# Threshold attention and a squared-ReLU layer on one core: own step orders for the first three attention periods, and another place for the unread transposes

## The chip, the cores and the metric

The kernel runs on one core of one Trainium2 chip. The metric is the device time of one execution in microseconds. Three timed runs of the kernel before gave 1300.67, 1300.70 and 1300.83 us, median 1300.7.

## The reference

The inputs are q, k and v of shape (8, 8, 576, 64), a threshold tau of 0.02, and two weight matrices, which arrive as 64-bit floats. All else is fp32.

```python
scores = (1 / sqrt(64)) * q @ k.T
thresh = max(scores, axis=-1) - tau
scores = where(scores >= thresh, scores, -1e9)
attn = exp(scores - max(scores));  attn /= sum(attn) + 1e-9
x = (attn @ v) transposed to (8*576, 8*64)          # 4608 x 512
h = maximum(x @ w_in, 0)                            # w_in: 512 x 2048
out = (h * h) @ w_out                               # w_out: 2048 x 512
```

## The kernel before

The program has three stages, one after the other: attention (to about 504 us), the layer with w_in (L827) and the layer with w_out (L962). The two layers multiply with seven block products on two levels instead of eight, and PE is their pace. The change lies in the first stage alone.

**Units and periods.** Batch and pair of heads give 32 pairs. Four blocks of 128 query rows and, for two pairs together, one of 64 + 64 rows make 144 units; a period handles two units, A and B, so periods 0 to 71 have scores, and the loop runs some on either side. The steps of a period are named by short words, and a list of these words is the order in which they are recorded (the loop `for name in CONVERTING if converts(p) else PLAIN`, L697). Every engine takes its instructions in the recorded order, and semaphores hold an instruction until what it needs is there; no scheduler moves anything (`tc.manual_schedule()`). Periods 0 and 1 use PLAIN; CONVERTING holds from period 2, while the weights are turned from 64 to 32 bits, chunk by chunk.

**The steps.** In the order in which one unit's data goes through them:

- T: PE transposes queries or keys of a later pair into two PSUM banks (L397); eT: ACT copies them out (L402, L410).
- SA, SB: PE's score products (L434), those of unit A with the 64 last keys of both units, and those of unit B, into banks of the tile `sc`.
- topA1 and the like: DVE copies the scores to SBUF and finds each row's extreme (the sign is turned with the queries) (L452); two per unit, one for each head. The text calls them tops.
- leastA, leastB: POOL adds tau (L459). powA0 and the like: ACT's exponential (L462). maskA0 and the like: DVE drops what is under the threshold and sums the rest (L467).
- over (POOL, L474), inv (DVE, L477), spread (POOL, L517): the reciprocal of the sum, widened for a transposition.
- V, U, W: PE transposes the attention weights (L379) of the period before or of the one before that; eV, eU, eW: ACT copies them out (L524).
- PV: PE's product with v (L533); x, xs: DVE, ACT and POOL scale and copy it (L640, L642, L657), and SP writes it to DRAM (L579).
- fetch and c1 to c6: SP's load of a weight chunk (L191) and its conversion: ACT (L205, L211), POOL (L218, L245), DVE (L226, L234).

**Banks.** `sc` has six PSUM banks, the tile `pt` the other two. T writes bank 1 and bank 4 of `sc`, where the scores of the last 64 keys lie as well, W writes banks 2 and 3. A helper, `touch`, makes two engines that use the same bank wait for each other in recorded order, and frees those that use different ones. `pt` has one buffer, so each use of it waits until the one before has been copied out.

**Unread transposes.** `keep_busy(times)` (L1008) records transposes of the identity into a new `pt` tile that nobody reads (L1013). There are 15 before the first queries are transposed, 8 before the first keys are, and 20 after period 0. The 8 and the queries before them share `pt`, and so the 8 wait until ACT has copied the queries out.

**Loads.** SP issues nearly all DMAs, in recorded order; each one waits for the one eight before it. A load of keys of a later pair is recorded with eT, behind the transposes that free its buffer.

Of the kernel before, what the change touches and what calls it, by code (L numbers as in the profile page):

```python
# [10 lines left out]
FP32 = mybir.dt.float32  # L11
# [37 lines left out]
def kernel(  # L49
# [25 lines left out]
    nc = tc.nc  # L75
    B, H, S, D = q.shape
    P = 128
# [7 lines left out]
    BANK = 512  # L85
# [19 lines left out]
    ident = const.tile([P, P], FP32, name="ident")  # L105
# [375 lines left out]
    def do(n, what, *args):  # L481
        if n in soft:
            soft[n][what](*args)
# [4 lines left out]
    for g in range(2, 2 * len(pairs)):  # L488
        two, x = divmod(g - 4, 4)
# [9 lines left out]
    def fill(m, f, pt, at=None):  # L499

        first, count = FILLS[f]
        if m not in wT:
            wT[m] = sb.tile([P, (2 * CH + 2) * P], FP32, tag="wT", bufs=W_RING, name="wT")
        for i, (u, c) in enumerate(FIRST[first : first + count]):
            half_turn(pt, i, weights[2 * m + u][:, c, :, :].rearrange("p j d -> p (j d)"), at)
        if f == "W":
            for j in range(2):
                half_turn(pt, count + j, wT[m][:, ts(SCALE_AT + j, P)], at)

    def widen(m):  # L510

        if m not in wT:
            wT[m] = sb.tile([P, (2 * CH + 2) * P], FP32, tag="wT", bufs=W_RING, name="wT")
        one = smalls.pop(m)[:, 3, 0:1]
        wide = bass.AP(tensor=one.tensor, offset=one.offset, ap=[one.ap[0], [1, 2], [2, 2], [0, D]])
        to = wT[m][:, ds(SCALE_AT * P, 2 * P)].rearrange("p (j u d) -> p j u d", j=2, u=2)
        nc.gpsimd.tensor_copy(out=to, in_=wide)  # L517
# [42 lines left out]
    def has(n):  # L560
        return 0 <= n < NU
# [22 lines left out]
    def converts(p):  # L584
        return is_wide and (has_chunk(p) or has_chunk(p - 1))

    def has_chunk(p):
        return p in starts

    def begun(n):  # L590
        return starts.get(n)

    PLAIN = """
        fetch U SA topA1 over s1 s2 topA0 SB topB1 inv eU powA1 V topB0 leastA spread PV powA0 maskA1 leastB maskA0 eV T powB1 x maskB1 powB0 xs maskB0 eT W eW
    """.split()
    CONVERTING = """
        fetch c1 T SA topA1 c3 topA0 U eU powA1 SB topB0 over topB1 powA0 c4 powB0 PV eT inv leastA maskA1 x powB1 leastB spread V eV maskA0 W maskB0 c5 c6 eW maskB1 xs c2
    """.split()

    def spots():  # L600
        return [(sc[:, ds(b * BANK + REST, (FULL + 1) * HALF)], b * BANK) for b in (1, 4)]

# [3 lines left out]
    def period(p):  # L606

        A, B_, a, b = 2 * p, 2 * p + 1, 2 * p - 2, 2 * p - 1
        m, turns = p - 2, TURNS.get(p, ())
        late, pt = {"W": []}, {}  # L610

        def fills(f, m):
            if has(2 * m):
                pt[f] = pt_pool.tile([P, 2, BANK], FP32, tag="pt", name="pt")
                fill(m, f, pt[f])

        def evict(f, m):
            if has(2 * m):
                filled(m, f, pt[f], 2 * BANK if f == "W" else None)

        def W():
            if has(2 * m + 2):
                pt["W"] = middle()
                fill(m + 1, "W", pt["W"], 2 * BANK)

        def turn_some():
            late["turn"] = [turn(g // 2, g % 2, spots()) for g in turns]

        def PV():
            if has(2 * m):  # L630
                values(m)

        def given_out():
            if has(2 * m):
                x = sb.tile([P, 2, P], FP32, tag="x", bufs=2, name="x")
                by_vector = (0,)
                for j in range(2):
                    by = sc[:, ds(5 * j * BANK, P)], wT[m][:, ts(SCALE_AT + j, P)]
                    if j in by_vector:
                        made = nc.vector.tensor_tensor(out=x[:, j, :], in0=by[0], in1=by[1], op=ALU.mult)  # L640
                    else:
                        made = nc.scalar.copy(x[:, j, :], by[0])  # L642
                    touch("x", made, 5 * j * BANK, P, m)
                late["x"] = x, [j for j in range(2) if j not in by_vector], wT[m]
                wT.pop(m)
                valued(m)

        def scaled_x():
            if has(2 * m):
                x, js, by = late["x"]  # L650
                if len(js) == 2:
                    nc.gpsimd.tensor_tensor(
                        out=x[:, :, :].rearrange("p j q -> p (j q)"), in0=x[:, :, :].rearrange("p j q -> p (j q)"),
                        in1=by[:, ds(SCALE_AT * P, 2 * P)], op=ALU.mult,
                    )
                for j in js if len(js) == 1 else ():
                    nc.gpsimd.tensor_tensor(out=x[:, j, :], in0=x[:, j, :], in1=by[:, ts(SCALE_AT + j, P)], op=ALU.mult)  # L657
                give_x(m, x)
            ask(False)

        def scored_a():
            if has(A):
                scores(A, False)
                scores(A, True)
                scores(B_, True)
                softmax(A)

        def scored_b():
            if has(A):
                scores(B_, False)  # L670
                softmax(B_)

        def every(key):
            for then in late.get(key, ()):
                then()

        steps = {
            "U": lambda: fills("U", m), "V": lambda: fills("V", m + 1), "W": W, "T": turn_some,
            "eU": lambda: evict("U", m), "eV": lambda: evict("V", m + 1), "eW": lambda: evict("W", m + 1),
            "eT": lambda: every("turn"),  # L680
            "SA": scored_a, "SB": scored_b,
            "PV": PV, "x": given_out, "xs": scaled_x,
            "c1": lambda: convert1(begun(p)), "c2": lambda: convert2(begun(p)),
            "c3": lambda: convert3(begun(p - 1)), "c4": lambda: convert4(begun(p - 1)),
            "c5": lambda: convert5(begun(p - 1)), "c6": lambda: convert6(begun(p - 1)),
            "s1": lambda: sums_due(p) and sums_step(), "s2": lambda: sums_due(p) and p % 2 == 0 and sums_step(), "fetch": lambda: fetch(begun(p + 2)),
        }
        steps["spread"] = lambda: has(2 * m + 2) and widen(m + 1)
        steps["over"] = lambda: do(a, "over")
        steps["inv"] = lambda: do(a, "inverse")  # L690
        for letter, n in (("A", A), ("B", B_)):
            for what, name in (("least", "least"),):
                steps[what + letter] = lambda n=n, name=name: do(n, name)
            for what, name in (("top", "top"), ("pow", "power"), ("mask", "mask")):
                for j in range(2):
                    steps[f"{what}{letter}{j}"] = lambda n=n, name=name, j=j: do(n, name, j)
        for name in CONVERTING if converts(p) else PLAIN:  # L697
            steps[name]()
        for n in (A, B_):
            if has(n) and units[n][1] == FULL:  # L700
                for i in units[n][0]:
                    turned.pop(i)
# [301 lines left out]
    with tc.manual_schedule():  # L1004
        with ExitStack() as stack:
            sc = stack.enter_context(tc.tile_pool(name="sc", bufs=1, space=PSUM)).tile([P, 6 * BANK], FP32, name="sc")
            pt_pool = stack.enter_context(tc.tile_pool(name="pt", bufs=1, space=PSUM))

            def keep_busy(times):

                pt = pt_pool.tile([P, 2, BANK], FP32, tag="pt", name="idle")
                for _ in range(times):
                    nc.tensor.transpose(pt[:, 0, 0:P], ident[:, :], ident[:, :])  # L1013

            load_q(0)
            load_k(0)
            read_tau()
            first = sb.tile([P, 4, 4], FP32, tag="small", bufs=4, name="small")
            nc.scalar.activation(out=first[:, 0, :], in_=ident[:, 0:4], func=AF.Exp)
            load_v(0)  # L1020
            keep_busy(15)
            pq = pt_pool.tile([P, 2, BANK], FP32, tag="pt", name="pq")
            turn(0, 0, [(pq[:, r, :], None) for r in range(2)])()
            keep_busy(8)
            turn(0, 1, spots(), nc.vector.tensor_copy)()
            for i in range(1, 3):
                load_v(i)
            for p in range(-2, NU // 2 + 3):
                period(p)
                if p == 0:  # L1030
                    keep_busy(20)
                if X_FIRST <= p < X_FIRST + 4:
                    load_x(0, XPARTS[p - X_FIRST :][:1])
                if p == X_FIRST + 4:
                    summing.append(prepare_x(0, lambda op, out, x, y: op(nc.gpsimd, out, x, y)))
            for _ in range(60):
                sums_step()
            ask()
# [186 lines left out]
```

## Time and profile before

One execution was profiled. Its own time is 1300.85 us, its span from the first to the last instruction 1299.1 us.

| | PE | PEld | DVE | ACT | POOL |
|---|---|---|---|---|---|
| busy us | 1260.8 | 1124.5 | 996.1 | 854.3 | 909.0 |
| share of the span | 97% | 87% | 77% | 66% | 70% |

PE is TensorE's matmuls and transposes, PEld its weight loads, DVE the vector engine, ACT the scalar engine, POOL GpSimd and SP the engine that issues DMAs. In rows of groups and of the order of time, the number in brackets is the engine's idle time before the row and what released it. A product of fp32 operands shows two records in the trace, a transpose one. The clock column is the share of TensorE's full speed that the throttle granted; it shows 1.00 ahead of the first record of the clock, which stands at 13.75 us, whatever the speed was there.

### The profile page before, as it was taken

To read this page: it belongs to the slowest core of one execution; us is meant where nothing else is said; L and a number is where in the kernel's file an instruction comes from. 1 tells how busy PE (TensorE), PEld (TensorE's weight loads), DVE (VectorE), ACT (ScalarE), POOL (GpSimd) and SP (SyncE) were. 2 spreads that over 40 slices of the span, in tenths; PEclk is the share of its full clock that TensorE was granted. 3 is DMA by queue.
4 is the path that set the end of the run, shared out by engine and by line. 5 is a ranking of instruction groups with operands and counts; after the bars stand their busy time and mean duration, and the time that the engine had idled before them with its cause. 6 is when DMAs were issued, how large, how long until landed. Compare 5 with 4: busy or idle time off the path is not lost.

```text
span 1299.1 us, 46337 instructions
## 1 busy us (share of the span) xinstructions
PE 1260.8 (97%) x18619; PEld 1124.5 (87%) x18619; DVE 996.1 (77%) x2425; ACT 854.3 (66%) x1536; POOL 909.0 (70%) x1102
## 2 busy tenths in 40 slices
PE   7999999999999999999999999999999999999998
PEld 4666666666766668999999999999999999999998
DVE  4999999999999995877787778777646654665463
ACT  4999999999999994757675766575523432343240
POOL 1566565566666663977897789768777867777775
PEclk8999999999999999999999999999999999999999
DMA  5465567534433322556655665479645324522411
GB/s 139 121 164 151 155 193 193 152 92 102 96 80 88 88 61 69 170 183 221 199 167 184 214 209 166 160 273 396 219 160 163 94 74 159 163 81 88 159 34 33
DMA packets 247031, 192.03 MB, mean 148 GB/s; under 512 B 97184, under 2 KB 195488, under 8 KB 246816
## 3 DMA queue, kind: packets, MB, share of 16 engines
q1 hardware_dynamic: 245360, 188.63, 48.2%
q8 instruction: 146, 2.39, 0.8%
q14 instruction: 69, 0.57, 0.2%
q10 hardware_dynamic: 1456, 0.44, 0.1%
HBM read 116.65 MB, written 72.35 MB: 145 GB/s over the span
## 4 chain that ended last, share of the span: by engine, by line
PE 60%; DMA 2%; ACT 1%; DVE 0%; issue 0%; POOL 0%; ACTq 0%; SPq 0%
PE ph L827 29%; PE po L962 29%; DMA wall<-w 1%; PE sc L533 1%; PE sc L434 1%; DMA g<-arena 0%; PE pt L379 0%; ACT arena L806 0%; ACT arena L807 0%; DVE arena L452 0%; POOL arena L122 0%; ACT arena L524 0%; ACT c L773 0%; DVE arena L467 0%; PE sc L379 0%
## 5 line engine op out<-in xcount | busy, mean ns | idle before, releaser
L125 POOL TENSOR_TENSOR arena<-arena 128x512 f32<-128x512 f32 (+1 forms) x314 | 377.6, 1221 | 124.7 <-DVE arena L125 110.1
L962 PE MATMUL po<-wall,arena 128*128 128x128 f32 x3528 | 394.7, 275 | 1.4 <-ACT arena L739 1.4
L962 PEld LDWEIGHTS po<-wall,arena 128*128 128x128 f32 x3528 | 394.2, 192 | 1.8 <-ACT arena L739 1.8
L827 PE MATMUL ph<-arena,wall 128*128 128x128 f32 x3528 | 394.2, 275 | 0.5 <-DVE arena L640 0.5
L827 PEld LDWEIGHTS ph<-arena,wall 128*128 128x128 f32 x3528 | 394.0, 192 | 0.6 <-ACT arena L642 0.6
L125 DVE TENSOR_TENSOR arena<-ph,arena 128x512 f32<-128x512 f32 x378 | 256.4, 689 | 86.3 <-PE ph L827 65.9
L122 POOL TENSOR_TENSOR arena<-arena 128x128 f32<-128x128 f32 (+2 forms) x314 | 254.6, 812 | 50.9 <-DMA arena<-w 34.6
L462 ACT ACTIVATE arena<-arena 128x576 f32<-128x576 f32 x288 | 223.0, 850 | 23.3 <-DVE arena L452 23.1
L125 DVE TENSOR_TENSOR arena<-po,arena 128x128 f32<-128x128 f32 x378 | 108.3, 290 | 168.1 <-PE po L962 164.0
L467 DVE SCALAR_TENSOR_TENSOR arena<-arena 128x576 f32<-128x576 f32 x288 | 227.1, 817 | 2.7 <-POOL arena L459 2.0
L452 DVE TENSOR_SCALAR_CACHE_REDUCE arena<-sc 128x576 f32<-128x576 f32 x288 | 203.9, 750 | 19.8 <-ACT arena L524 7.1
L773 ACT COPY c<-arena 128x512 f32<-128x512 f32 (+1 forms) x303 | 173.6, 580 | 49.8 <-DVE arena L122 41.3
L533 PEld LDWEIGHTS sc<-arena 64*64 64x64 f32 x5760 | 144.7, 133 | 47.5 <-DVE arena L452 44.6
L122 DVE TENSOR_TENSOR arena<-arena,c 128x512 f32<-128x512 f32 (+1 forms) x267 | 174.9, 663 | 5.7 <-ACT c L773 4.0
L434 PE MATMUL sc<-arena 64*64 64x64 f32 (+1 forms) x2304 | 171.5, 422 | 5.2 <-ACT arena L402 3.4
L533 PE MATMUL sc<-arena 64*64 64x128 f32 (+1 forms) x5760 | 160.7, 262 | 12.8 <-DVE arena L452 9.4
L524 ACT COPY arena<-pt 128x1024 f32<-128x1024 f32 x144 | 156.4, 1086 | 5.2 <-PE pt L379 5.1
L739 ACT COPY arena<-po 128x128 f32<-128x128 f32 x63 | 16.6, 264 | 186.5 <-PE po L962 183.7
L379 PEld LDWEIGHTS pt<-ident,arena 64*128 64x128 f32 x2304 | 83.4, 139 | 43.2 <-ACT arena L524 34.5
L739 ACT COPY arena<-ph 128x512 f32<-128x512 f32 x63 | 36.6, 581 | 122.6 <-PE ph L827 122.0
L434 PEld LDWEIGHTS sc<-arena 64*64 64x64 f32 x2304 | 60.9, 135 | 55.0 <-issue 28.4
L379 PE MATMUL pt<-ident,arena 64*128 64x64 f32 x2304 | 101.2, 228 | 3.8 <-ACT arena L524 3.3
(47 smaller groups left out, 944.3 us busy)
## 6 DMA issues: line engine op xcount, KB each, us to landing
g<-arena SPq DMA_DIRECT2D x144, 256.0 KB, 2.4
arena<-g SPq DMA_DIRECT2D x144, 256.0 KB, 4.5
w<-arena SPq DMA_DIRECT2D x60, 256.0 KB, 2.3
wall<-w SPq DMA_DIRECT2D x49, 256.0 KB, 5.3
arena<-w SPq DMA_DIRECT2D x44, 256.0 KB, 4.1
arena<-in_v_dram SPq DMA_DIRECT2D x32, 288.0 KB, 3.8
out_dram<-arena SPq DMA_DIRECT2D x70, 128.0 KB, 2.2
arena<-in_q_dram SPq DMA_DIRECT2D x64, 128.0 KB, 3.8
```

The source lines that it names most:

```text
L122: e.tensor_tensor(out=out, in0=x, in1=y, op=ALU.subtract)
L125: e.tensor_tensor(out=out, in0=x, in1=y, op=ALU.add)
L379: made = nc.tensor.transpose(pt[:, r, ts(slot, HALF)], of[rows, :], ident[rows, rows])
L434: made = nc.tensor.matmul(sc[at, ds(to, count)], lhs, kT[rows, ds(at_k, count)], start=True, stop=True)
L452: made = nc.vector.tensor_scalar(out=s[:, j, :], in0=sc[:, ds(at, S)], scalar1=1.0, scalar2=None, op0=ALU.mult, op1=ALU.min, accum_out=nmx ...
L462: nc.scalar.activation(out=w[:, :, j, :], in_=of(j), func=AF.Exp, bias=nmx[:, j : j + 1], scale=-1.0)
L467: nc.vector.scalar_tensor_tensor(out=w[:, :, j, :], in0=of(j), scalar=thr[:, j : j + 1], in1=w[:, :, j, :], op0=ALU.is_le, op1=ALU.mult, a ...
L524: touch("weights", nc.scalar.copy(joined(to), whole(pt, 0, count)), at, 2 * BANK, m)
L533: made = nc.tensor.matmul(sc[ds(u * D, D), ds(5 * j * BANK + row, count)], loaded_v[i][rows, (c - (u != j)) % CH, :], wT[m][rows, ds(weigh ...
L773: nc.scalar.copy(c, y)
L827: nc.tensor.matmul(to[:, j, :], W_IN[m, k][:, ts(j, P)], of[k][:, m - 1, :], start=(not more and j == 0), stop=True, skip_group_check=True,)
L962: nc.tensor.matmul(to, g[:, j, :], w[:, j, :], start=(not more and j == 0), stop=(j == 3), skip_group_check=True)
```

## The change

The first three periods get lists of their own (`FIRSTS`). The words id4, id8 and id14 are new steps that record so many unread transposes inside a period, in a `pt` tile; the lists use id4 and id14 in period 0 and id4 twice in period 1. The 20 after period 0 are gone. In the opening, the unread transposes go to bank 2 of `sc` (`unread`) instead of `pt`: 15 as before, 6 in place of 8, and 4 new ones between the first keys' transposes and period 0.

In the lists themselves: periods 0 and 1 record T ahead of the period's last top (the old list has it behind unit A's masks), period 1 records SB ahead of the second top and the weight load last instead of first, period 2 records c2 near its start and c1 at its end instead of the reverse, and the masks and thresholds stand in other orders. No other period changes, and the same work is done in each.

```diff
+    FIRSTS = {
+        0: """
+            SA SB id4 fetch topA1 topA0 powA1 leastA powA0 topB1 T id14 powB1 topB0 powB0 eT maskA0 leastB maskA1 maskB1 maskB0
+        """.split(),
+        1: """
+            SA topA1 SB topA0 id4 topB0 over inv powA1 V eV spread T powA0 topB1 eT W id4 leastA maskA1 leastB powB1 maskA0 maskB1 powB0 maskB0 fetch eW
+        """.split(),
+        2: """
+            T SA fetch c2 U topA1 c3 over eU SB powA1 topA0 c4 powA0 c5 topB0 powB0 leastA topB1 eT maskA1 PV inv powB1 V leastB x spread maskA0 eV maskB1 maskB0 W eW xs c6 c1
+        """.split(),
+    }
...
+        for times in (4, 8, 14):
+            steps[f"id{times}"] = lambda times=times: keep_busy(times)
...
-        for name in CONVERTING if converts(p) else PLAIN:
+        for name in FIRSTS.get(p) or (CONVERTING if converts(p) else PLAIN):
...
-            def keep_busy(times):
+            def keep_busy(times, to=None):
 
-                pt = pt_pool.tile([P, 2, BANK], FP32, tag="pt", name="idle")
+                if to is None:
+                    to = pt_pool.tile([P, 2, BANK], FP32, tag="pt", name="idle")[:, 0, 0:P]
                 for _ in range(times):
-                    nc.tensor.transpose(pt[:, 0, 0:P], ident[:, :], ident[:, :])
+                    nc.tensor.transpose(to, ident[:, :], ident[:, :])
+
+            unread = sc[:, ds(2 * BANK, P)]
...
-            keep_busy(15)
+            keep_busy(15, unread)
             pq = pt_pool.tile([P, 2, BANK], FP32, tag="pt", name="pq")
             turn(0, 0, [(pq[:, r, :], None) for r in range(2)])()
-            keep_busy(8)
+            keep_busy(6, unread)
             turn(0, 1, spots(), nc.vector.tensor_copy)()
+            keep_busy(4, unread)
...
                 period(p)
-                if p == 0:
-                    keep_busy(20)
```

## The prediction

> **What bounds the kernel now.** I read the page's shares first, then a table of stages whose bounds are the starts of the first maximum ("top", L452) of each attention period, then the order of time in the first 37 us on PE and on DVE, and last the clock records.
>
> ```profile
> PE 1260.8 (97%) x18619; PEld 1124.5 (87%) x18619; DVE 996.1 (77%) x2425; ACT 854.3 (66%) x1536; POOL 909.0 (70%) x1102
> ...
> 12.47:19.76 7.29, 5.73 (x64) 3.24 (x60) 5.85 (x17) 3.63 (x6) 1.31 (x3) 1.00 0.99 279
> 19.76:28.28 8.52, 5.38 (x78) 3.01 (x72) 5.82 (x18) 5.54 (x10) 1.71 (x4) 0.75 0.40 99
> 28.28:36.43 8.15, 7.96 (x170) 5.65 (x168) 6.73 (x17) 6.84 (x12) 3.50 (x5) 0.84 0.05 12
> 36.43:43.30 6.87, 6.53 (x161) 4.64 (x160) 6.87 (x21) 6.87 (x14) 2.26 (x5) 1.00 0.52 137
> 43.30:50.17 6.87, 6.25 (x158) 4.46 (x154) 6.87 (x23) 6.87 (x14) 4.23 (x8) 1.00 0.50 129
> ```
>
> In the stage rows the columns are length, then busy time on PE, PEld, DVE, ACT, POOL, then the granted clock. From period 3 (36.43) each period lasts 6.87 us and DVE and ACT are busy for all of it: the pace is set there, and whatever moves 36.43 moves everything behind it. Periods 0, 1 and 2 last 7.29, 8.52 and 8.15 us with 5.8, 5.8 and 6.7 us of DVE work: the slack is here alone.
>
> ```profile
> 1.34 3.46 PE L1013 MATMUL idle<-ident 128*128 128x128 f32 x15 [1.34 <-POOL ident masks.py:199]
> 6.60 1.97 PE L1013 MATMUL idle<-ident 128*128 128x128 f32 x8 [1.05 <-ACT arena L402]
> 8.50 0.80 PE L397 MATMUL sc<-ident,arena 64*128 64x64 f32 x10
> 10.01 3.99 PE L434 MATMUL sc<-arena 64*64 64x512 f32 x32 [0.71 <-ACT arena L402]
> 15.56 0.46 PE L397 MATMUL sc<-ident,arena 64*128 64x64 f32 x8 [1.56 <-DVE arena L452]
> 15.96 2.40 PE L1013 MATMUL idle<-ident 128*128 128x128 f32 x20
> 18.29 2.18 PE L434 MATMUL sc<-arena 64*64 64x512 f32 x32
> 22.68 0.59 PE L397 MATMUL sc<-ident,arena 64*128 64x64 f32 x10 [1.56 <-DVE arena L452]
> 25.10 0.69 PE L397 MATMUL sc<-ident,arena 64*128 64x64 f32 x8 [1.58 <-ACT arena L402]
> 25.72 2.41 PE L434 MATMUL sc<-arena 64*64 64x512 f32 x24
> 34.59 1.32 PE L434 MATMUL sc<-arena 64*64 64x512 f32 x24
> ```
>
> ```profile
> 12.47 0.76 DVE L452 TENSOR_SCALAR_CACHE_REDUCE arena<-sc 128x576 f32<-128x576 f32 x1 [2.61 <-PE sc L434]
> 19.76 0.76 DVE L452 TENSOR_SCALAR_CACHE_REDUCE arena<-sc 128x576 f32<-128x576 f32 x1 [1.29 <-issue]
> 28.28 0.76 DVE L452 TENSOR_SCALAR_CACHE_REDUCE arena<-sc 128x576 f32<-128x576 f32 x1 [2.70 <-issue]
> 31.14 0.76 DVE L452 TENSOR_SCALAR_CACHE_REDUCE arena<-sc 128x576 f32<-128x576 f32 x1 [1.42 <-ACT arena L462]
> ```
>
> The same 32 score records take 3.99 us at 10.01 and 2.18 at 18.29, and 24 of them 2.41 at 25.72 and 1.32 at 34.59: twice PE runs at half speed. The clock records say when: full from 13.75, half from 23.99 (the 0.75 and 0.84 above), full from 30.82, half again at 1297.16. All lie on one grid of 3.41 us (10.24 and 6.83 apart). Counting PE's busy share in each grid window from the order of time: full after the windows ending at 13.75 and 30.82 (both 1.00 busy); not after 0.64, 0.67, 0.79 and 0.67; half after 0.40 (20.58 to 23.99) and 0.38 (1293.75 to 1297.16); held after 0.54 (13.75 to 17.16) and everything above. Sliding such a window over 36 to 1293 us finds no share under 0.54, so a shift brings no new drop there.
>
> **The change part by part.** The sum is against the profiled execution: 1300.85 us, span 1299.1 and 1.75 around it, 0.15 above the median. Waits of the new order are read from the built program, durations from the rows.
>
> *Before the first top.* The six unread transposes wait for nothing; the eight waited 1.05 us for the queries' copy. 15 take 3.46 and 8 take 1.97, so one is 0.213 and six take 1.54: from 5.48 to 7.02 at half clock. The keys' transposes follow at 6.95 instead of 8.50 (the last of their loads landed at 6.05): 1.55 earlier. The copies stay. Then four unread transposes stand before the first scores, waiting for the very copies that the scores wait for: no gap is filled, they are pure delay, 4 x 0.213 + 0.2 = 1.05 at half clock, about 0.55 at full (20 in 2.40: 0.12 each). Scores to first top: 2.46 at half (10.01 to 12.47), 1.47 at full (18.29 to 19.76). At half, the top is at 10.01 - 1.55 + 1.05 + 2.46 = 11.97, a gain of 0.5. If the clock is full from 6.92, the keys' transposes also save 0.23, and it is 8.23 + 0.55 + 1.47 = 10.25, a gain of 2.2. Which one is the large unknown: the new window 3.51 to 6.92 is nearly all busy, but with transposes only.
>
> *Period 0.* 20 unread transposes become 4 + 14, and the turn T now stands ahead of the last top. It writes the bank that this top reads, so T waits for the third top and the last top for T: DVE stands 0.06 + 0.46 + 0.07, about 0.55. Tops 4 x 0.68, masks 4 x 0.74: 2.72 + 0.55 + 2.96 = 6.24. The next scores are ready in time: T ends 2.6 after the first top, 14 transposes take 1.7, scores to top 1.47, together 5.8. So 7.29 becomes 6.24: 1.05 (0.8 if its scores still run at half, third top 0.23 later).
>
> *Period 1.* T again precedes the last top: 0.6 on DVE. 2.72 + 0.6 + 2.96 = 6.3. The path to the next scores: last top ends 3.5 after the first, ACT's copies of the keys end 0.7 later, the queries' turn takes 0.41, scores to top 1.32 + 0.14: 6.1, hidden. At half clock it is 4.2 + 0.69 + 2.41 + 0.14 = 7.45 and shows. So 8.52 becomes 6.35 (2.15) or 7.45 (1.05). The two fours of this period stand where PE waits for masks or copies anyway; if that cover is gone, each costs about 0.55. SP's weight load moves from first to last, past six key loads, some 5 us later: it lands near 25, its reader (ACT, period 3) comes near 29, and nothing else waits. POOL's widened scale moves ahead of one threshold (0.40 against a mask 0.7 later): nothing.
>
> *Period 2.* Floor on DVE: 2.72 + 0.09 + 0.20 + 2.96 = 5.97; ceiling the old 8.15. In the old one the idle 1.42 was the second scores at half clock, and three masks took 0.98, 1.00 and 1.15 instead of 0.81 beside POOL's L657 and L218, 0.7 in all. L657 stays beside the masks, L218 now waits for the conversion's first ACT step, which moves from the front to the end of the period (and lies before DVE's step that needs it by about a microsecond). I take half of that excess: 6.6 at full clock, 6.95 at half: 1.55 or 1.2.
>
> **The rivals.**
> - A, full from 6.92 and held: 2.2 + 1.05 + 2.15 + 1.55 = 6.95, 1293.9.
> - B, full from 6.92, but half again at 20.58: 2.2 + 1.05 + 1.05 + 1.2 = 5.5, 1295.4. The new window 17.16 to 20.58 holds the value transposes' end, T, the weights' transposes and four unread ones, 1.6 to 1.8 us: 0.47 to 0.53, between the 0.40 that dropped and the 0.54 that held. I take B a little over A, since the gaps are exactly there.
> - C, transposes don't raise the clock, full from 13.75 as now, no later drop (the windows are 0.7 busy or more): 0.5 + 0.8 + 2.15 + 1.55 = 5.0, 1295.85. For it: no window of transposes alone has raised the clock in this trace. Against it: the window 13.75 to 17.16 held at 0.54 with 0.07 of score matmuls, and 1293.75 to 1297.16 dropped at 0.38 with matmuls alone, so transposes do count for holding.
> - D, as C with a drop in period 2: 0.5 + 0.8 + 1.05 + 1.2 = 3.55, 1297.3.
> - E, nothing reaches the end, within 0.2% (2.6 us, about what a measurement of this kernel tells from no change): a wait in period 3 takes it back. Against it, DVE and ACT have no idle time in the periods from 36.43 on, and the key loads that period 3 reads near 27 landed by 21.56.
> - F, slower: with unread transposes on its path PE stays at half clock until 27.4 or later. Then 14 of them take 3.2, period 0 lasts 3.3 + 3.2 + 2.46 less overlap, 8.5, period 1 as much, period 2 8.15: 11.97 + 8.5 + 8.5 + 8.15 = 37.1, 0.7 late, 1301.5; period 3 at half adds 1.3 and period 4 as much, 1304.1. It decides if no window before 27.4 counts as full, against the two that did.
>
> [...]
>
> **How the numbers follow.** A 0.24, B 0.29, C 0.26, D 0.09, E 0.07, F 0.05. The likeliest is B: 1300.85 - 5.5 = 1295.4. The range takes in A with the rest of the masks' excess gone (1293.9 - 0.7 = 1293.2) and D with both fours of period 1 uncovered (1297.3 + 1.1, say 1298.2). Faster by over 0.2%: A to D, 0.88; within, E and half of F's first step, 0.08; slower 0.04.
>
> **What would show it.** First top at 10.3 (A, B) or 12.0 (C, D); a clock record at 6.92 or none before 13.75; a gap on DVE of about 0.6 before the last top of periods 0 and 1; steps of 6.2 to 6.5, 6.35 or 7.45, and 6.6 to 7; then 6.87 from period 3, and the 809 us behind 490 (1299.1 - 490) unchanged. Wrong would be a period 3 that is longer than 6.87, a second drop, or a grid that lies elsewhere against the program's start.

## The result and the profile after

The changed kernel takes 1295.95 us (median of nine executions, 1292.89 to 1299.07), the kernel before beside it 1300.67 us; the ratio is 0.9961 (0.9950 to 0.9972). The forecast was 1295.4 with a range from 1293.2 to 1298.2. The nine executions differ by 6.2 us. The three of the kernel before that are shown ahead of the forecast differed by 0.16 us, but the nine beside the changed kernel differ by 3.8 us (1299.20 to 1302.98), so the kernel before varies too. One of the 67 executions of the kernel before that were timed beside the experiments took 1561.58 us at a mean clock of 0.753, a slow state, and is left out of every comparison below.

One execution was profiled. It took 1293.22 us, its span is 1291.4 us, so it is 7.63 us shorter than the profiled one of before. The first line is that of shares on the page. Below it is the table of stages, with bounds at the first tops of periods 0 to 5; the columns are as before (length, busy time on PE, PEld, DVE, ACT, POOL, granted clock, and then DMA's share and rate).

```profile
PE 1259.7 (98%) x18627; PEld 1124.3 (87%) x18627; DVE 996.2 (77%) x2425; ACT 855.5 (66%) x1536; POOL 909.8 (70%) x1102
...
9.32:15.59 6.27, 5.75 (x66) 3.26 (x58) 5.77 (x17) 3.64 (x6) 1.09 (x2) 1.00 0.68 200
15.59:22.09 6.50, 4.95 (x86) 3.43 (x84) 5.89 (x20) 5.61 (x10) 1.69 (x4) 1.00 0.69 156
22.09:28.78 6.69, 6.67 (x164) 4.93 (x162) 6.47 (x19) 6.33 (x12) 2.65 (x5) 1.00 0.48 148
28.78:35.80 7.02, 6.90 (x164) 4.83 (x160) 6.95 (x21) 7.02 (x14) 2.92 (x6) 1.00 0.54 135
35.80:42.67 6.87, 6.43 (x154) 4.46 (x150) 6.87 (x21) 6.87 (x13) 4.24 (x8) 1.00 0.51 131
```

The first top comes at 9.32 instead of 12.47, and the periods last 6.27, 6.50 and 6.69 us instead of 7.29, 8.52 and 8.15: 3.15 + 1.02 + 2.02 + 1.46 = 7.65 us. From the first top of period 3 to the end it is 1262.65 us, before 1262.64, so in these two executions the whole of it arrives at the end. PE's busy time is 1259.7 instead of 1260.8, with eight more weight loads and matmuls in the count: the work is the same, it stands closer together, and at full speed.

The order of time on PE, and two rows of the one on DVE:

```profile
1.34 3.46 PE L1028 MATMUL sc<-ident 128*128 128x128 f32 x15 [1.34 <-POOL ident masks.py:199]
5.33 0.88 PE L1028 MATMUL sc<-ident 128*128 128x128 f32 x6
6.14 0.53 PE L397 MATMUL sc<-ident,arena 64*128 64x64 f32 x10
7.38 0.63 PE L1028 MATMUL sc<-ident 128*128 128x128 f32 x4 [0.71 <-ACT arena L402]
7.93 2.18 PE L434 MATMUL sc<-arena 64*64 64x512 f32 x32
11.89 1.75 PE L1028 MATMUL idle<-ident 128*128 128x128 f32 x14
13.57 2.18 PE L434 MATMUL sc<-arena 64*64 64x512 f32 x32
20.59 1.32 PE L434 MATMUL sc<-arena 64*64 64x512 f32 x24
```

```profile
11.94 0.76 DVE L452 TENSOR_SCALAR_CACHE_REDUCE arena<-sc 128x576 f32<-128x576 f32 x1 [0.50 <-PE sc L397]
18.39 0.76 DVE L452 TENSOR_SCALAR_CACHE_REDUCE arena<-sc 128x576 f32<-128x576 f32 x1 [0.60 <-PE sc L397]
```

Every score row of 32 takes 2.18 us, that of 24 takes 1.32: no product of this stage ran at half speed. The clock's records are full from 5.25 and half only at 1292.07, behind the last product. The window that ended at 5.25 is this (a table of two stages with the same bounds; the first row counts the unread transposes alone, for PE and PEld, the second all instructions):

```profile
1.84:5.25 3.41, 2.96 (x14) 2.56 (x13) 1.00 0.78 169
...
1.84:5.25 3.41, 3.41 (x22) 3.06 (x21) 0.04 (x1) 0.99 (x1) 0.00 (x0) 1.00 0.78 169
```

PE was busy for all of the 3.41 us, 2.96 us of it with unread transposes and the rest with the queries' transposes. No product of data had run yet, and behind this window the clock was full.

The window's place is the other difference. Before, the records lay at 13.75, 23.99, 30.82 and 1297.16, the last three 3, 5 and 376 times 3.4133 us behind the first; here they lie at 5.25 and 1292.07, 377 times 3.4133 apart, and 13.75 - 5.25 is 2.49 windows. In the other profiles of this study the first record is at 4.22 to 13.47 in nearly any phase, and two executions of one kernel (the combined one below) have it at 5.88 and at 4.82. So the grid isn't tied to the program's start: each execution has a phase of its own, that is, another place of the grid against that start.

What the phase can do is seen in period 1, the thinnest stretch behind the first full window. Here a window of the grid lies at 15.49 to 18.90 and is 0.64 busy, and the clock held. At the worst phase the share would be 0.55, in this window:

```profile
15.85:19.26 3.41, 1.86 (x33) 1.35 (x32) 2.81 (x10) 2.78 (x5) 0.81 (x4) 1.00 0.78 153
```

Each timed execution also has its mean granted clock: 1.000, 1.000, 1.000 at 1292.89, 1293.22, 1293.75; 0.999 at 1295.52, 1295.95, 1296.65; 0.997 at 1298.02, 1298.65, 1299.07. One window at half speed lowers the mean by 0.5 x 3.41 / 1292 = 0.0013, so these three groups lost no window, about one, about two. The groups are rough: the mean takes the time ahead of the first record as full, whatever the speed was (it is 1.000 in a profile below whose first scores take 4.12 us), and counts the end behind the last product (half from 1297.16 to 1299.07 in the profile of before, 0.0007).

The groups fit the phase as a cause of the spread, but not as all of it. Their medians lie 2.7 us apart, and a window at half speed takes at most 0.5 x 3.41 = 1.7 us of PE's work (an estimate from the window's length). And the 53 executions of the kernel before that share a mean clock of 0.996 or 0.997 still range from 1298.11 to 1305.13. How much of the 6.2 us is the phase's isn't shown.

### The profile page after: what moved, and what is told of

It reads as the page before. It is cut to its first block, busy times and chain, and to the rows that moved or that the text cites. A ratio compares the mean times of both kernels' runs of the same rounds, so it can differ in the third digit from the quotient of the medians.

```text
span 1291.4 us, 46350 instructions
## 1 busy us (share of the span) xinstructions
PE 1259.7 (98%) x18627; PEld 1124.3 (87%) x18627; DVE 996.2 (77%) x2425; ACT 855.5 (66%) x1536; POOL 909.8 (70%) x1102
## 4 chain that ended last, share of the span: by engine, by line
PE 61%; ACT 1%; DVE 1%; DMA 0%; issue 0%; POOL 0%; ACTq 0%; DVEq 0%; POOLq 0%
PE ph L841 30%; PE po L976 29%; PE sc L533 1%; PE sc L434 1%; DMA g<-arena 0%; ACT c L787 0%; ACT arena L820 0%; ACT arena L821 0%; PE pt L379 0%; ACT arena L524 0%; DVE arena L452 0%; DVE arena L125 0%; DVE arena L122 0%; POOL arena L122 0%; DVE arena L467 0%
## 5 line engine op out<-in xcount | busy, mean ns | idle before, releaser
L462 ACT ACTIVATE arena<-arena 128x576 f32<-128x576 f32 x288 | 228.4, 889 | 21.2 <-DVE arena L452 21.2
L434 PE MATMUL sc<-arena 64*64 64x64 f32 (+1 forms) x2304 | 168.0, 414 | 4.6 <-ACT arena L402 2.7
L524 ACT COPY arena<-pt 128x1024 f32<-128x1024 f32 x144 | 161.7, 1123 | 2.0 <-PE pt L379 1.9
```

The source lines that it names most:

```text
L434: made = nc.tensor.matmul(sc[at, ds(to, count)], lhs, kT[rows, ds(at_k, count)], start=True, stop=True)
L462: nc.scalar.activation(out=w[:, :, j, :], in_=of(j), func=AF.Exp, bias=nmx[:, j : j + 1], scale=-1.0)
L524: touch("weights", nc.scalar.copy(joined(to), whole(pt, 0, count)), at, 2 * BANK, m)
```

## The experiments

Unless another kernel is named, each is the changed kernel with the edit shown. The unread transposes write nothing that is read, so kernels without them compute the same. The first four ran on one chip beside a kernel before with a median of 1301.10 us, the next four (from the changed kernel again to the one without the 21) on another beside 1300.52, the last three and the second sample of the combined kernel on a third beside 1301.39. Kernels of different chips are best compared by their distance to the kernel before: the changed kernel lies 4.7 us below it in its first nine executions and 3.9 in its second sample. "P3" below is the first top of period 3 (28.78 above).

### The unread transposes inside the periods left out

```diff
-            SA SB id4 fetch ... topB1 T id14 powB1 ...
+            SA SB fetch ... topB1 T powB1 ...
-            SA topA1 SB topA0 id4 topB0 ... W id4 leastA ...
+            SA topA1 SB topA0 topB0 ... W leastA ...
```

> The changed kernel without the unread transposes inside periods 0 and 1 (id4, id14, id4, id4); the lists and the opening stay. Theory 1 (the clock, which these transposes hold, and the lists each bring a part): a window of PE's busy share falls near or under 0.5 between 17 and 24 us at most phases of the clock's grid, period 2 runs at half clock, steps of periods 1 and 2 near 7.2 and 7.0 instead of 6.5 and 6.7: 0.5 to 1.5 us above the changed kernel, about 1297. Theory 2 (the lists alone bring the gain, the transposes are idle work): the same as the changed kernel, within 0.3 us, or a little faster. Theory 3 (the transposes alone bring it): back near the kernel before, with the gain of the opening only, about 1298.5.

1296.55 us (1295.20 to 1298.50, eight), ratio 0.9967 (0.9956 to 0.9979). The stages of period 0, of period 1, of period 2, and a window of the clock's grid:

```profile
9.62:15.89 6.27, 4.17 (x50) 1.34 (x42) 5.77 (x17) 3.63 (x6) 1.09 (x2) 1.00 0.73 219
15.89:23.28 7.39, 5.12 (x72) 3.18 (x72) 5.98 (x20) 5.62 (x10) 1.91 (x5) 0.77 0.79 214
23.28:30.07 6.79, 6.77 (x164) 4.97 (x164) 6.47 (x17) 6.18 (x11) 2.40 (x4) 1.00 0.16 37
16.22:19.63 3.41, 1.19 (x27) 0.91 (x26) 2.80 (x10) 2.74 (x5) 0.79 (x4) 1.00 0.64 120
```

PE is busy for 1.19 of 3.41 us (0.35) in a window of period 1, and behind it the clock is half for one window, 19.64 to 23.05. Period 0 is as long as with its 18 unread transposes, so there they lay beside other work; period 1 is 0.89 longer and period 2 0.10. That is the price of one dropped window here, 1.0 us. These rows fit the first theory. The median doesn't tell it from the second: 4.6 us below the kernel before, against 4.7 and 3.9 for the changed kernel, so what the words in the periods are worth in the median isn't shown.

### The opening as it was

```diff
-            keep_busy(15, unread)
+            keep_busy(15)
-            keep_busy(6, unread)
+            keep_busy(8)
-            keep_busy(4, unread)
```

> The changed kernel with the opening of before: 15 and 8 unread transposes in the tile pt, none ahead of the first scores. Theory 1: the first top goes back from 9.3 to about 12.4 us (the scores start near 10 and mostly run at half clock), the later steps stay 6.3 to 6.6: 1.5 to 2.5 us above the changed kernel, about 1298. Theory 2: the same 1.5 to 2.5 above. Theory 3: most of the gain gone, 1299.5 or more. If the opening is hidden, no difference.

1300.12 us (1294.55 to 1302.13, twelve), ratio 0.9988 (0.9975 to 1.0000). Most of the gain is gone, as the third theory had it. The profiled execution is the quickest of the twelve: full from 4.93 and no drop, first top 10.12, P3 29.59, so the gap in the opening costs 0.8 in the good case. Only two of the twelve have a mean clock of 1.000; nine lie at 1299.3 or above, and none of those was profiled. What the opening's unbroken row of transposes buys is thus more than the 0.8 that it shortens the way to the first top, and it lies in executions that this profile doesn't show. The raise that this opening got late in the kernel before (13.75) is the likely cause, but it is argued, not shown; the mean clock can't show it, since it takes the time ahead of the first record as full.

### The new opening with the old lists

```diff
-        for name in FIRSTS.get(p) or (CONVERTING if converts(p) else PLAIN):
+        for name in CONVERTING if converts(p) else PLAIN:
                 period(p)
+                if p == 0:
+                    keep_busy(20)
```

> The changed kernel's opening with the step orders of before (PLAIN, CONVERTING) and the 20 unread transposes after period 0. Theory 1: first top near 9.5, but steps of 8.5, 8.4 and 6.5 to 7.5 as PE waits for masks and copies and falls to half clock in period 1 or 2: 1.5 to 3 us under the kernel before, about 1298.5. Theory 2: nearly as slow as before, 1300 or more. Theory 3: as fast as the changed kernel, 1296.

1298.38 us (1297.01 to 1304.47, twelve), ratio 0.9990 (0.9977 to 1.0003). Periods 0 to 2, and two windows of the grid:

```profile
9.47:18.12 8.65, 6.59 (x64) 4.80 (x60) 5.75 (x16) 3.54 (x6) 1.32 (x3) 0.80 0.83 247
18.12:26.65 8.53, 5.38 (x78) 3.01 (x72) 5.82 (x18) 5.53 (x10) 1.71 (x4) 0.77 0.52 126
26.65:34.87 8.22, 8.15 (x170) 5.81 (x168) 6.74 (x17) 6.85 (x12) 3.51 (x5) 0.82 0.05 12
9.08:12.49 3.41, 1.35 (x32) 0.47 (x26) 3.02 (x9) 2.22 (x4) 0.42 (x2) 1.00 0.40 84
19.32:22.73 3.41, 1.00 (x24) 0.72 (x20) 3.41 (x12) 3.41 (x6) 1.48 (x3) 1.00 0.34 67
```

The early full clock (5.66) is there, but the old lists lose it twice, behind windows of 0.40 and 0.29 busy, and their 20 unread transposes stand on the path at half speed: period 0 is 8.65 us, longer than in the kernel before. The opening's 3.0 us on the first top have shrunk to 1.6 at P3 (34.87 against 36.43). Neither half of the change is clear of the kernel before by its ratio (both intervals reach 1.0000), and both together are; the rows say why the opening needs the lists: a raised clock is worth what they keep of it.

### Without the four ahead of the first scores

```diff
             turn(0, 1, spots(), nc.vector.tensor_copy)()
-            keep_busy(4, unread)
```

> The changed kernel without the four unread transposes ahead of the first scores, which wait for the copies that the scores wait for. As the prediction has it, they are pure delay: first top 0.5 to 0.6 us earlier at full clock (near 8.8 instead of 9.3), 1295.4. Rival: they fill the window in which the clock is judged, and without them it drops more often or is full later: no gain, 1296 to 1297.

1296.59 us (1296.00 to 1297.03, five), ratio 0.9966 (0.9953 to 0.9979). First top 8.74, 0.58 earlier than in the changed kernel's profile (at another phase); the forecast priced the four at 0.55. The stages of period 1, and two windows that follow one another:

```profile
15.01:23.40 8.39, 6.84 (x80) 4.34 (x78) 5.98 (x20) 5.74 (x10) 1.92 (x5) 0.71 0.74 203
15.15:18.56 3.41, 1.94 (x35) 1.43 (x31) 2.80 (x10) 2.71 (x4) 0.90 (x3) 1.00 0.84 183
18.56:21.97 3.41, 3.33 (x27) 2.16 (x31) 3.03 (x10) 3.02 (x6) 1.02 (x2) 0.50 0.52 130
```

The drop comes behind a window that is 1.94 / 3.41 = 0.57 busy, and the next one, 0.98 busy, doesn't raise the clock; two windows are lost and P3 is at 31.05. From the first top to P3 it is 22.31 us against 19.46 in the changed kernel's profile: two windows cost 2.85 here, more than twice the 1.0 above. Had the program run 0.58 later, as with the four, this window would have held what stands at 14.57 to 17.98, which is 2.52 / 3.41 = 0.74 busy; that the clock would then have held is argued. Whether the four help on average these five don't say.

### The changed kernel again

> The changed kernel once more, unaltered, to see another phase of the clock's grid. Theory 1 (each execution has its own phase, and the time depends on whether a grid window falls on the thin stretch of period 1): times spread over 1292.9 to 1299 again, and the profiled one has either no drop and a first maximum of period 3 near 28.8, or a half-speed stretch that begins between 18.5 and 21 and that maximum at 30 to 32. Theory 2 (the phase was an accident of the first visit, and the grid is tied to the program's start): the first record of the clock at 5.25 again, no drop, 1293.2 with a spread under 0.5.

1296.61 us (1293.19 to 1299.25, eleven), ratio 0.9972 (0.9961 to 0.9983). The spread is back. The first record of the profiled execution lies at 5.19, next to the 5.25 of the other one, so this profile shows no other phase; the two of the combined kernel do. Put together, the 20 executions have a median of 1296.5 us; six with a mean clock of 1.000 have a median of 1293.5, seven at 0.998 to 0.999 one of 1295.95, seven at 0.996 to 0.997 one of 1298.65. Of the 66 executions of the kernel before that were timed beside these experiments, 53 lie at 0.996 or 0.997.

The profiled one adds something else. It took 1296.35 us with no drop, and P3 at 28.74, the same start as the one at 1293.22. It lost 3.2 us later: 1.25 in period 30 (8.39 instead of 7.14), and 1.64 in the layer with w_in (395.56 from the start of its first product to that of its last instead of 393.92, with PE standing 0.34 and 0.76 us near 610 us). The order of time on PE in period 30:

```profile
223.31 0.61 PE L397 MATMUL sc<-ident,arena 64*128 64x64 f32 x8
225.08 0.35 PE L397 MATMUL sc<-ident,arena 64*128 64x64 f32 x2 [1.17 <-DMA arena<-in_q_dram]
```

T waits 1.17 us for the last load of queries, which SP issued at 221.87 here and at 219.92 in the other execution; why it came late isn't shown. In three other profiles (the combined kernel's first, the one with T late and the one without unread transposes) the layer with w_out is longer by 1.2 to 1.4 us (397.13 to 397.30 instead of 395.88), also at full clock. So the phase isn't the only thing that varies: late loads and waits in the layers cost an execution a microsecond or more each.

### Four more in the thin stretch of period 1

```diff
-            ... V eV spread T powA0 topB1 ...
+            ... V eV spread T id4 powA0 topB1 ...
```

> The changed kernel with four more unread transposes behind T in period 1, where PE stands 0.84 for a mask. Theory 1 (the drop in the thin window of period 1 is what the slower executions pay): no window of 3.41 us before 30 is under 0.7 busy at any phase, so no half-speed stretch behind the first full one, the executions near 1298 to 1299 are gone, median 1293.5 to 1295, first maximum of period 3 at 28.5 to 29.5. Theory 2 (the spread comes from elsewhere, say from when the loads land): the spread stays 6 us and the median at 1296.

1296.51 us (1293.98 to 1297.95, seven), ratio 0.9966 (0.9953 to 0.9980): no better in the median, as the second theory had it. In its profile the mechanism of the first is there: the thin window of period 1 is 0.79 busy (at no phase under 0.77, against 0.55 in the changed kernel), no drop before 250, P3 at 28.86. So drops in period 1 aren't all that the changed kernel's median pays for. But T waits 1.29 us for queries in period 30, and then comes a drop where I had not looked, at 254.70. The window ahead of it and the one at half speed:

```profile
251.29:254.70 3.41, 1.94 (x44) 1.43 (x44) 3.41 (x10) 2.83 (x7) 1.24 (x2) 1.00 0.33 70
254.70:258.12 3.42, 3.42 (x34) 1.02 (x27) 1.47 (x6) 1.86 (x3) 2.92 (x5) 0.50 0.52 145
```

This is the stretch behind the last chunk of weights, whose last step on DVE is at 250.5. A window that falls there is 0.57 busy and drops; in the changed kernel's second profile one lay a little otherwise, was 0.63 busy, and held.

### The combined kernel: those four, and the opening's four off the path

```diff
-            ... V eV spread T powA0 topB1 ...
+            ... V eV spread T id4 powA0 topB1 ...
-            keep_busy(4, unread)
+            keep_busy(4)
```

> As the one with four more behind T in period 1, and the four unread transposes ahead of the first scores go into a tile of their own pool instead of the bank of the scores, so that they run while ACT copies the keys and not behind it. Theory 1 (the four were delay of about 0.5, and the window of period 1 is full enough): 0.5 below the other one, median 1292.5 to 1294.5, first top near 8.8, first maximum of period 3 near 28.2. Theory 2 (the four buy a held clock in a window of the opening, so that taking them off the path gains nothing, as leaving them out gained nothing): the same median as the other one, within 0.5.

> The combined kernel once more, for comparison on the same chip with the other three and for a second sample: median 1294 to 1295 and a ratio of 0.995 to 0.9965, if its lead over the changed kernel (1294.4 against 1296.0 and 1296.6) is no accident of a few executions; 1296 or more, if it is.

1294.41 us (1292.97 to 1297.63, six), ratio 0.9955 (0.9940 to 0.9970), and 1294.97 us (1293.70 to 1299.83, eleven), ratio 0.9956 (0.9944 to 0.9969). The order of time on PE in the second one's opening:

```profile
6.73 0.66 PE L1028 MATMUL idle<-ident 128*128 128x128 f32 x4 [0.23 <-ACT arena L402]
7.32 2.18 PE L434 MATMUL sc<-arena 64*64 64x512 f32 x32
```

In a tile of the other pool the four wait 0.23 for the queries' copy instead of 0.71 for the keys', run while ACT copies the keys, and the scores start 0.6 earlier (0.3 in the first one). First tops are at 9.01 and 8.70, P3 at 28.46 and 28.18, the windows of period 1 0.79 busy. Eleven of the 17 executions have a mean clock of 1.000, against six of 20 of the changed kernel, and the median of the 17 is 1294.57 against 1296.5. It has the lowest median here in both samples, but its lead isn't certain: the intervals of the ratios overlap, and drawing the 17 and 20 executions again at random puts the 1.9 us between 0.2 and 3.6. On the same chip its first sample lies 2.1 below the kernel of the section before, where 0.5 was expected; the rows give 0.3 to 0.6 of that, and the rest is open.

### Without the 21 of the opening

```diff
-            keep_busy(15, unread)
-            keep_busy(6, unread)
```

> The changed kernel without the 15 and the 6 unread transposes of the opening (they write nothing that is read). Theory 1 (windows of transposes alone raise the clock, and these 21 buy it): no full window before the first scores, so the first record of the clock at 9 to 12.5, the first scores at half speed for 2.5 to 4 us, first top at 10.6, 1.3 later than in the profiled execution of the changed kernel; median about 1 us above the changed kernel, 1297. Theory 2 (only products raise it, and the 21 are in the way): first top earlier than 9.3 and median under 1295.5.

1295.61 us (1295.07 to 1296.35, five), ratio 0.9961 (0.9948 to 0.9973). The order of time on PE:

```profile
5.42 1.10 PE L397 MATMUL sc<-ident,arena 64*128 64x64 f32 x10 [0.33 <-DMA arena<-in_k_dram]
7.20 1.09 PE L1028 MATMUL sc<-ident 128*128 128x128 f32 x4 [0.68 <-ACT arena L402]
8.21 4.12 PE L434 MATMUL sc<-arena 64*64 64x512 f32 x32
```

The steps are as expected: first scores at half speed, 4.12 us, first top at 10.70 and first record at 13.47 (later than the 9 to 12.5 named). But the median isn't above the changed kernel's. Its start costs 1.4 on the first top and 0.5 in period 0 (6.81), P3 is at 30.70, and yet four of the five have a mean clock of 1.000 (in which the half speed ahead of 13.47 doesn't count). So the 21 transposes do buy an early clock, worth 1.9 at P3 in undisturbed executions, and bring no lower median: without them it is 1.0 lower on the same chip (1295.61 against 1296.61). That with them many executions lose a window again would explain it and is argued from the mean clocks alone. Five executions are few.

### T behind the last top of period 0 (on the combined kernel)

```diff
-            ... topB1 T id14 powB1 topB0 powB0 eT ...
+            ... topB1 id14 powB1 topB0 T powB0 eT ...
```

> The combined kernel (four more behind T in period 1, the four of the opening off the path), and in period 0 T moved behind the last top. Theory 1 (the last top of period 0 waits 0.5 for T alone, and the next scores have room): the gap on DVE goes, period 0 lasts 5.7 to 5.8 instead of 6.26, median about 0.5 below the combined kernel, 1293.9. Theory 2 (the next scores set the end of period 0, the gap is cover only): period 0 stays at 6.2 to 6.3, the idle time moves ahead of the next first top, median as the combined one.

1296.34 us (1294.01 to 1297.25, five), ratio 0.9961 (0.9946 to 0.9976). The stage of period 0, and the wait that stays in period 1:

```profile
8.96:14.63 5.67, 5.61 (x66) 3.12 (x58) 5.67 (x15) 3.65 (x6) 1.09 (x2) 1.00 0.51 139
```

```profile
17.44 0.76 DVE L452 TENSOR_SCALAR_CACHE_REDUCE arena<-sc 128x576 f32<-128x576 f32 x1 [0.60 <-PE sc L397]
```

The gap in period 0 is gone, period 0 lasts 5.67 with DVE busy throughout, and P3 is at 27.83, the earliest of all profiles. The median shows none of it: the profiled execution then waits 1.42 us for queries in period 30 and loses a window at 253.39, behind one that is 0.57 busy.

### The old list for period 2 (on the combined kernel)

> The combined kernel, with period 2 in the old list. Theory 1 (the old period 2 was long because its second scores ran at half speed and its masks lay beside POOL's converters, and the new list takes about half of that excess away): at full speed the old list gives 6.7 to 7.0 against 6.68, so the new list of period 2 is worth 0 to 0.3 and the clock the rest. Theory 2 (the order of the new list is what shortened period 2): 7.5 or more with the clock full, median 0.8 or more above the combined kernel.

```diff
     FIRSTS = {
         0: ...
         1: ...
-        2: """
-            T SA fetch c2 U topA1 c3 over eU SB ... W eW xs c6 c1
-        """.split(),
```

1295.25 us (1293.22 to 1299.60, seven), ratio 0.9957 (0.9942 to 0.9973). Periods 2 and 3:

```profile
22.15:29.04 6.89, 6.88 (x170) 4.98 (x166) 6.74 (x19) 6.53 (x12) 3.52 (x6) 1.00 0.43 128
29.04:35.91 6.87, 6.50 (x156) 4.52 (x152) 6.87 (x23) 6.87 (x14) 2.26 (x5) 1.00 0.51 131
```

At full clock the old list takes 6.89 against 6.69, but period 3 then lasts 6.87 instead of 7.02: 13.76 against 13.71 for both. The new list of period 2 is worth nothing that can be told. In period 3 of the changed kernel ACT is busy for all of the 7.02 us, and its first copy of transposed weights (L524) starts 0.80 us behind the first top instead of 0.60, behind two steps c1 (L205) in a row: c1, moved to the end of period 2, is what makes period 3 longer, as far as these rows show.

This profile loses a window too, far behind the changed periods: half from 491.33 to 494.74, at the end of the attention stage, behind this one, 0.53 busy:

```profile
487.91:491.33 3.42, 1.83 (x52) 1.47 (x44) 2.82 (x10) 2.75 (x5) 1.49 (x4) 1.00 0.16 31
```

Every profile of this study, that of before included, has windows of 0.53 or 0.54 there at some phase.

### No unread transposes at all

```diff
-            keep_busy(15, unread)
-            keep_busy(6, unread)
-            keep_busy(4, unread)
-            ... id4 ... id14 ...
-            ... id4 ... id4 ...
+            the same lists without these words
```

> The changed kernel with no unread transposes at all (47 that write nothing that is read are left out). Theory 1 (the unread transposes are needed: without them no window before 27 is full and the clock stays at half, the case that my forecast called F): periods 0 and 1 at 7.3 to 8.5, first maximum of period 3 at 33 to 37, median 1298.5 to 1301. Theory 2 (the new orders bring PE close enough together by themselves, the scores raise the clock within period 0 or 1): first record of the clock at 12 to 17, first maximum of period 3 at 29 to 31, median 1295 to 1296.5, no worse than the changed kernel.

1298.46 us (1295.30 to 1300.74, eleven), ratio 0.9979 (0.9968 to 0.9990). The edit leaves out 51 unread transposes (15 + 6 + 4 in the opening, 18 in period 0, 8 in period 1; PE's count falls from 18627 to 18576), not the 47 that the expectation names. In the profile the scores alone raise the clock at 10.11, it drops at 20.35 behind a window that is 0.36 busy, period 1 lasts 7.32, P3 is at 30.30. The start follows the second theory, the median lies at the lower end of the first. So F, the case of a clock that stays at half, doesn't come even without any unread transpose. This kernel lies 2.9 us below the kernel before, the changed one 4.7 and 3.9: together the 51 are worth about 1 to 2 us, less than half of the change's gain. The rest comes with the new orders, and with the 43 unread transposes of before gone from their places.

## Why the prediction was right, and where it wasn't

**The total was right, the case wasn't one case.** 1295.4 was worked out for B: full clock early, one window lost in period 1. The profiled execution is A, full and held, for which the forecast had 1293.9; it took 1293.22. The median, 1295.95, is near B's number because the kernel does A, B and worse in turn: by their mean clocks about a third of 20 executions each lost no window, one, or two. That it came within 0.6 us of the forecast is in part luck, since late loads and waits that the forecast doesn't have lengthen some executions as well.

**The step that failed** is that windows were placed: "All lie on one grid", from which the forecast took raises at 6.92 and 13.75 and a drop at 20.58. Within one execution the records do (10.24 and 6.83 apart, 3 and 2 windows of 3.413), but each execution has another phase, and what the text gave as last among the things that would make it wrong, "a grid that lies elsewhere against the program's start", is what the profiles show: first records at 4.22, 4.82, 4.91, 5.19, 5.25, 5.53, 5.66, 5.88, 5.98 and 6.64 in ten profiles with the same 15 transposes from 1.34. Three executions of before that agreed within 0.16 us had hidden it. With it fell "a shift brings no new drop there", said of all that lies behind 36 us: three profiles lose a window at 253.39, 254.70 and 491.33, behind windows that are 0.57, 0.57 and 0.53 busy. And B's window in period 1 was put at 0.47 to 0.53; in the profile of the changed kernel it is 0.55 at the worst phase and was 0.64.

**The opening.** A's term was 2.2, measured 3.15. The six unread transposes wait for nothing, as said (their row at 5.33 shows no wait); with the clock full from 5.25 instead of 6.92 they take 0.88 us where the forecast had 1.54 and the keys' transposes start at 6.14, not at 6.95. That is 0.8 of the 0.95. The four cost about 0.58 on the first top, forecast 0.55.

**C fell.** Transposes do raise the clock, shown by the window of 1.84 to 5.25: transposes alone, 1.00 busy, and the clock full behind it. C's sum was 5.0; by rows it was 7.65.

**Period 0**: 1.05 forecast, 1.02 measured; the gap ahead of the last top 0.55, measured 0.50, and moving T took it away. **Period 1**: 2.15 or 1.05; 2.02 with the clock held, and 8.52 - 7.39 = 1.13 in the profile with one window lost. The gap of 0.6 is 0.60. **Period 2**: 1.55, measured 1.46, but for another reason than half of the masks' excess: the clock does it, the old list gives 8.15 - 6.89 = 1.26 of it, and of the 0.20 of the new order 0.15 go back in period 3 (7.02, not the 6.87 that the forecast held to be unmoved). A period 3 longer than 6.87 was among the things named as wrong; it is longer by 0.15.

**B's threshold.** Drops behind 0.29, 0.35, 0.36 and 0.40 fit the forecast, that behind 0.53 lies where it left the matter open; 0.57 should have held. B's price, one window, is 0.89 + 0.10 = 1.0 by the profile without the words; the forecast had 1.10 in period 1 and 0.35 in period 2. Period 2 hardly pays there; in the kernel without the four ahead of the first scores, which lost two windows, periods 1 and 2 pay 2.85 together.

**E and F.** Nothing is taken back where E looked for it, in period 3's waits for keys; but in period 30 late queries take 1.2 to 1.4 us in three of the profiles. F didn't come in any.

## What to carry to other kernels

Where a gain hangs on the clock's windows, work it out for all phases of the grid, and take a mean: a profile shows one phase, and a few executions that agree don't show that it is fixed. Unread work is worth placing where it fills a gap that a window can fall into, and on no path; with the four taken off the path and four more in the thin stretch the quick case was the more common one (11 of 17 executions at a mean clock of 1.000, against 6 of 20). After that, what is won at the start competes with drops and late loads further back, and a profile that stops at the changed periods would not show it.

## What the runs showed of the hardware

- Transposes alone raised the clock: in the changed kernel it was full at 5.25 behind a window 1.00 busy (2.96 us of 3.41 with unread ones of 128 x 128, the rest with the queries'), and with T late at 4.22 behind a window whose busy time is 2.87 us (0.84), all with unread ones.
- The share of PE's busy time doesn't settle when the clock drops. Windows of 0.57 dropped three times (15.15 without the four; 251.29; 249.97 with T late) and one of 0.53 once (487.91 with the old list for period 2), while one of 0.54 held in the kernel before (13.75) and one of 0.57 with the old opening (4.93). Nor does it settle the raise: 0.84 (the one above) and 0.86 (scores alone, 6.70 to 10.11 without unread transposes) raised it, 0.84 (6.64 to 10.06 without the 21) and 0.98 (18.56 to 21.97 without the four) didn't. Nor does the share of transposes of 64 rows: they took 0.39 to 0.51 of the four windows of 0.53 and 0.57 that dropped, and with the old lists a window at 493.76 held that is 0.53 busy, 0.44 of the window with such transposes. What decides stays open.
- PE worked in every window ahead of a drop before 500 us: the longest time that it stood in one of them is 2.06 us of 3.41 (9.08 to 12.49 with the old lists).
- The granted clock's column is 1.00 ahead of the first record whatever the speed was: in the kernel without the 21, 32 score records took 4.12 us there.
